# Two loads moved down the transfer queue in a fused spectral-and-MLP kernel

## The chip, the cores and the metric

The kernel runs on one core of one Trainium2 chip. The metric is device time in microseconds (us) for one execution. Before the change, three runs took 409.81, 409.92 and 409.93 us; the median is 409.92 us.

A core has five instruction queues, each of which works strictly in its own order: TensorE (PE, matmuls; its weight loads are listed apart as PEld), VectorE (DVE), ScalarE (ACT), GpSimd (POOL) and SyncE (SP). SP computes nothing here. It issues the transfers, all of them on one DMA queue that 16 DMA engines serve.

## The reference, cut to what matters

With `S = 2048` tokens and `D = 448` channels, `F = 1792`:

```python
xn  = layernorm(x)
A   = irfft2(rfft2(xn) * (w_r + 1j*w_i))          # spectral filter
h   = gelu(layernorm(xn) @ w1)                     # [S, D]
hs  = concat(shift(h, +1, -1, +2, -2)) @ w2        # one shift per quarter of the channels
x1  = xn + hs
B   = x1 + gelu(layernorm(x1) @ w3) @ w4           # w3 [D, F], w4 [F, D]
out = x + A + B
```

All of it is in float32. The kernel keeps the accuracy by splitting each float32 operand into a high and a low float16 half and multiplying three of the four products.

## The kernel before, in words

The 2048 tokens are seen as 128 rows of 16 blocks (token = 16 a + b); a block b holds the 128 tokens of one b. Four groups of four blocks are worked through in the order `GRP = [[14, 15, 0, 1], [2, 3, 4, 5], [6, 7, 8, 9], [10, 11, 12, 13]]`. The text calls them groups 0 to 3, as the code does.

The first 95 us are the front of the kernel:

- `norm1` normalises the blocks of a group. Groups 0 and 1 are transposed by TensorE (`turn_pe`, line 410). Groups 2 and 3 are split into halves by ACT and DVE and transposed by DMA (`turn`, line 900: source `x`, target `w4x`).
- `w1_unit(g, i)` (line 477) multiplies one block by w1 (`w1_in`, line 465, eleven matmuls), applies gelu on ACT (line 486), writes the high half on ACT (line 488) and the low half on DVE (line 489) into one of a few buffers `hs`, and lets SP transpose it into `h` (line 492). The text calls this last one a turning transfer of h. The diff calls them ("h", g, i).
- `w2_mm` and `w2_tile` (lines 498 and 514) multiply four shifted quarters of h by w2 (line 510, three matmuls for each quarter) and DVE adds the result to x (line 517).
- w3 and w4 each need one power-of-two scale for the whole matrix. `squares` (line 242) sums their squares on ACT (line 246), `powers` (line 248) adds up on DVE (line 251, tile `pt`), sums over partitions by one small TensorE matmul (line 258, tile `pm`), and makes the scale on DVE (lines 261 to 264). Then `split_w` writes the two halves (ACT line 291, DVE line 292). For w3 the text calls the sum pt3 and the matmul pm3, for w4 pt4 and pm4.

w3 has 448 rows. Three loads of 128 rows (line 217) and one of 64 rows (line 219) bring it into `w3raw`; the 64 rows are copied once more into the other 64 partitions by a transfer from `w3raw` to `w3raw` (line 1039).

After the front come the MLP (`front`, line 764: matmuls at line 435; `back`, line 791: matmuls at lines 811 and 826), and beside it the spectral path. Its first stage is `do_fold` (line 571): it reads two blocks of the original x again (line 574) into one of four buffers in turn. The fourth buffer, used by the folds of blocks 6 and 14, is the tile `hgm`, which is free from the start; the other three come into being only when earlier pools close.

The order on each queue is not the order of the code. A list scheduler with its own cost estimates sets it when the program is built. `behind(key)` (line 399) binds what is issued inside it to come after the instructions recorded under that key; for two transfers on SP this fixes their order. The program waits for data by semaphores, which the build places.

The chain of w4 touches the change as well. `load_w4` (line 231) brings w4 in four pieces; pieces 2 and 3 are issued behind ("h", 3, 3). Group 3 has only three `hs` buffers (`HS = 3`), so that its fourth block writes the buffer of its first, after that one's turning transfer has landed.

Of the kernel before, what the change touches and what calls it, by code (L numbers as in the profile page):

```python
# [19 lines left out]
S, D, DF, F = 2048, 448, 225, 1792  # L20
# [102 lines left out]
def body(tc, nc, x, wf, w1, w2, w3, w4, c_g, c_n, c_small, out):  # L123
    V, A, P, T, SY = nc.vector, nc.scalar, nc.gpsimd, nc.tensor, nc.sync
# [28 lines left out]
    def bank(tag, name):  # L153
        return ps.tile([128, 512], F32, tag=tag, bufs=2, name=name)
# [14 lines left out]
    xv = x.rearrange("(a b) d -> a b d", b=NB)  # L169
# [25 lines left out]
    def load_x(g):  # L195
        if g:
            SY.dma_start(xt[g], xv[:, GRP[g][0]:GRP[g][0] + 4])
        else:
            for i in (0, 2):
                SY.dma_start(xt[g][:, i:i + 2], xv[:, GRP[g][i]:GRP[g][i] + 2])  # L200
# [13 lines left out]
    def load_w3(ts):  # L214
        for t in ts:
            if t < 3:
                SY.dma_start(w3raw[:, t], w3[128 * t:128 * t + 128])
            else:
                SY.dma_start(w3raw[0:64, 3], w3[384:448])

    load_w3([0, 1])
    load_x(3)
    load_w3([2, 3])
    cross = x2mem.bitcast(F32)[:, 4 * F:4 * F + 2 * D].rearrange("p (i n) -> p i n", i=2)
    x2all = x2mem[:, 0:8 * F].rearrange("p (j t n) -> p j t n", j=4, t=7)
    w4raw = x2mem.bitcast(F32)[:, F:].rearrange("p (f n) -> p f n", f=14)
# [169 lines left out]
    after = {}  # L396

    @contextlib.contextmanager
    def behind(*key):
        key = key if len(key) > 1 else key[0]  # L400
        with contextlib.ExitStack() as st:
            for i in after[key]:
                st.enter_context(tc.issue_after(i))
            yield
# [51 lines left out]
    def h_at(g, i):  # L456
        return 128 * i if g else 144 * i + 16

    def w1_in(g, units, ts, passes=range(3)):
        for p in passes:  # L460
            for t in ts:
                for i, pm in units:
                    wi, xi = ((0, 0), (0, 4), (4, 0))[p]
                    if t < 3 or p != 1:
                        m = T.matmul(pm[:, :D], xTs[g][:, xi + t, 128 * i:128 * i + 128], w1p[:, wi + t],  # L465
                                     start=t == 0 and p == 0, stop=t == 3 and p == 2)
        return m
# [9 lines left out]
    def w1_unit(g, i, pm=None):  # L477
        if pm is None:
            pm = bank(("tr" if g < 3 else "mm", "acc")[i // 2], f"pw1_{g}{i}")
            after["u", g, i] = (w1_in(g, [(i, pm)], range(4)).ins,)  # L480
        c = CS[GRP[g][i]]
        pm = pm[:, :D]
        pv_ = pm.rearrange("p (k n) -> p k n", k=4)
        h = hs_buf[c % (HS if g == 3 else HS + 2)]
        with behind(0, max(i - 2, 0)) if g == 0 and i else contextlib.nullcontext():
            A.activation(out=pm, in_=pm, func=AF.Gelu_apprx_tanh, scale=gsc[:, c:c + 1])
        with behind("a2") if g == 1 and i > 1 else contextlib.nullcontext():
            u = A.activation(out=h[:, 0, :, 0:112], in_=pv_, func=AF.Copy, scale=h1)
            v = V.scalar_tensor_tensor(out=h[:, 1, :, 0:112], in0=pv_, scalar=h1, in1=h[:, 0, :, 0:112],
                                       op0=ALU.mult, op1=ALU.subtract)  # L490
        o = h_at(g, i)
        d = SY.dma_start_transpose(out=hT[g][:, :, o:o + 128], in_=h.rearrange("p i k n -> p (i k n)"))
        after[g, i] = u.ins, v.ins
        after["h", g, i] = (d.ins,)
# [3 lines left out]
    def w2_mm(b, ks):  # L498
        if b not in w2b:
            w2b[b] = bank("mm" if b in (2, 3) else "sp", f"pw2_{b}")  # L500
        for k in ks:
            src, o = b - SHIFT[k], 1
            if src < 0:
                src, o = src + NB, 0
            elif src >= NB:
                src, o = src - NB, 2
            g, i = WHERE[src]
            o += h_at(g, i) - 1
            for hi, wi in ((0, 0), (0, 1), (1, 0)):
                m = T.matmul(w2b[b][:, :D], hT[g][:112, 4 * hi + k, o:o + 128], w2p[:, wi, k],  # L510
                             start=k == 2 and hi + wi == 0, stop=k == 3 and hi == 1)
        after["w2", b] = (m.ins,)
# [58 lines left out]
    def do_fold(b0):  # L571
        f = xf_buf[b0 // 2 % 4]
        X = f.rearrange("p b s d -> p (b s d)")[:, 0:2 * D + 2].rearrange("p (b d) -> p b d", b=2)
        after["X", b0] = (SY.dma_start(X[:, :, 0:D], xv[:, b0:b0 + 2]).ins,)
        with behind("f", *FOLD[b0 // 2]):
            for i in range(2):
                x_ = X[:, i, 0:D]
                A.activation(out=x_, in_=x_, func=AF.Identity, scale=xn_scale[b0 + i], bias=xn_bias[b0 + i])
            A.activation(out=X[:, :, D:D + 1], in_=X[:, :, 0:1], func=AF.Copy)  # L579
        ad = X[:, :, 0:D].rearrange("p b (h d) -> p h b d", h=2)[:, :, :, 0:113]  # L580
        bc = X[:, :, 1:D + 1].rearrange("p b (h d) -> p h b d", h=2)[:, ::-1, :, 223:110:-1]
        u = xr.rearrange("p (a b s d) -> p a b s d", a=2, b=2, s=2)
        P.tensor_tensor(out=u[:, 0], in0=ad, in1=bc, op=ALU.add)  # L583
        P.tensor_tensor(out=u[:, 1], in0=ad, in1=bc, op=ALU.subtract)
        for k, op in ((0, ALU.add), (2, ALU.subtract)):
            i = P.tensor_tensor(out=f[:, :, k:k + 2].rearrange("p b s d -> p s b d"), in0=u[:, :, 0], in1=u[:, :, 1], op=op)
        after["fold", b0] = (i.ins,)
        for i in range(2):
            folds[b0 + i] = f[:, i].rearrange("p s d -> p (s d)")
# [429 lines left out]
    turn(2)  # L1019
    for k in range(1, 4):  # L1020
        w1_unit(1, k)
    for b, ks in ((0, (2,)), (1, (2,)), (0, (0,)), (2, (2,)), (1, (0,)), (2, (0,)), (3, (2,))):
        w2_mm(b, ks)
    with behind("w2p"):
# [86 lines left out]
    for b in range(0, NB, 2):  # L1111
        do_fold(b)
        step1_in(b)
        step1_in(b + 1)
        with behind("m", *PACE[b // 2]):
            step1(b)
            step1(b + 1)
# [80 lines left out]
```

## Time and profile before

| what | value |
|---|---|
| median of three runs | 409.92 us |
| the profiled execution, its own time | 409.72 us |
| its span in the trace | 407.6 us |
| PE busy | 401.3 us (98%) |
| DVE busy | 304.2 us (75%) |
| ACT busy | 268.6 us (66%) |
| POOL busy | 179.8 us (44%) |
| DMA queue | 46.4% of 16 engines' span |
| granted TensorE clock | 0.999 |

The trace counts 2.1 us less than the execution's time, for what lies before the first and after the last instruction. A row of the timeline has the start in us, the duration in us, the engine, the line, the operation, the tiles as out<-in, how many instructions are merged, and in square brackets how long the engine stood idle before it and what released it. In the list of transfers the last number is the time from issue to landing. A row of the table of stretches gives for each engine its busy time in the stretch, then the granted clock, the share of the DMA engines and what they moved in GB/s.

### The profile page before, as it was taken

To read this page: it belongs to the slowest core of one execution; us is meant where nothing else is said; L and a number is where in the kernel's file an instruction comes from. 1 tells how busy PE (TensorE), PEld (TensorE's weight loads), DVE (VectorE), ACT (ScalarE), POOL (GpSimd) and SP (SyncE) were. 2 spreads that over 40 slices of the span, in tenths; PEclk is the share of its full clock that TensorE was granted. 3 is DMA by queue.
4 is the path that set the end of the run, shared out by engine and by line. 5 is a ranking of instruction groups with operands and counts; after the bars stand their busy time and mean duration, and the time that the engine had idled before them with its cause. 6 is when DMAs were issued, how large, how long until landed. Compare 5 with 4: busy or idle time off the path is not lost.

```text
span 407.6 us, 8828 instructions
## 1 busy us (share of the span) xinstructions
PE 401.3 (98%) x3379; PEld 296.0 (73%) x3379; DVE 304.2 (75%) x658; ACT 268.6 (66%) x465; POOL 179.8 (44%) x276
## 2 busy tenths in 40 slices
PE   8998999999999999999999999999999999999996
PEld 4553555666767777776888887877788888888885
DVE  5988999899653757894577777763488879889645
ACT  4698993884737865763488888785956566544332
POOL 3889723011197747499243344441231254217100
PEclk9999999999999999999999999999999999999999
DMA  8999999915910375317055666642000022323201
GB/s 282 351 274 198 177 180 261 260 23 109 207 48 0 92 233 175 103 36 170 19 135 146 151 145 151 153 112 60 2 2 2 24 68 75 108 70 112 92 2 45
DMA packets 57209, 49.46 MB, mean 121 GB/s; under 512 B 41312, under 2 KB 52192, under 8 KB 57168
## 3 DMA queue, kind: packets, MB, share of 16 engines
q1 hardware_dynamic: 57168, 48.91, 46.4%
q8 instruction: 26, 0.43, 0.5%
q14 instruction: 15, 0.12, 0.1%
HBM read 35.06 MB, written 3.67 MB: 95 GB/s over the span
## 4 chain that ended last, share of the span: by engine, by line
PE 96%; DMA 2%; ACT 1%; DVE 0%; issue 0%; ACTq 0%
PE pw L435 33%; PE acc L811 24%; PE pw L510 9%; PE pw L465 6%; PE cr L826 4%; PE acc L826 3%; PE pu L707 3%; PE ps L604 3%; PE pp L661 2%; PE pe L727 2%; PE px L678 2%; PE py L749 2%; PE wps L889 2%; DMA h<-hs 2%; PE pta L414 1%; PE end L811 1%
## 5 line engine op out<-in xcount | busy, mean ns | idle before, releaser
L435 PE MATMUL pw<-x2mem,w3p 128*128 128x256 f16 x1232 | 149.7, 272 | 0.0
L435 PEld LDWEIGHTS <-w3p 128*128 128x128 f16 x1232 | 118.7, 98 | 19.4
L811 PE MATMUL acc<-w4p,hf 128*128 128x448 f16 x508 | 107.4, 352 | 0.0
L811 PEld LDWEIGHTS <-hf 128*128 128x128 f16 x532 | 51.5, 98 | 35.5
L777 DVE SCALAR_TENSOR_TENSOR hf<-pw,h,hf 128x512 f16<-128x512 f32 x56 | 41.8, 747 | 36.5 <-ACT hf L776 36.3
L773 ACT ACTIVATE pw<-pw,pe 128x512 f32<-128x512 f32 x56 | 36.7, 656 | 44.8 <-PE pw L435 44.6
L510 PE MATMUL pw<-w2p,h 112*128 112x448 f16 x192 | 39.2, 353 | 1.3 <-DMA h<-hs 1.2
L734 POOL TENSOR_TENSOR e<-e 128x226 f32<-128x226 f32 x16 | 11.1, 696 | 63.7 <-ACT e L731 56.2
L776 ACT ACTIVATE hf<-pw,h 128x512 f16<-128x512 f32 x56 | 38.3, 683 | 1.3
L465 PE MATMUL pw<-w1p,w4x 128*128 128x448 f16 x176 | 34.8, 352 | 0.5 <-DVE h L967 0.5
L510 PEld LDWEIGHTS <-h 112*128 112x128 f16 x192 | 18.4, 98 | 18.0 <-DMA h<-hs 2.2
L688 POOL TENSOR_TENSOR xr<-te 128x450 f32<-128x450 f32 x16 | 15.7, 981 | 34.5 <-DVE te L686 34.5
L465 PEld LDWEIGHTS <-w4x 128*128 128x128 f16 x176 | 17.1, 98 | 16.4 <-ACT w4x L424 0.7
L696 POOL TENSOR_TENSOR zb<-xr,zb 128x450 f16<-128x450 f32 x16 | 16.1, 1009 | 16.8 <-ACT zb L695 16.8
L684 DVE SCALAR_TENSOR_TENSOR te<-px,sc,wc 128x450 f32<-128x450 f32 x16 | 11.0, 685 | 10.6 <-ACT te L683 7.0
L683 ACT ACTIVATE te<-px 64x450 f32<-64x450 f32 x32 | 17.2, 538 | 1.7 <-PE px L678 1.2
L719 ACT ACTIVATE U<-y 113x512 f16<-113x512 f16 x32 | 18.0, 620 | 0.1
L741 ACT ACTIVATE vh<-e 128x448 f16<-128x448 f32 x16 | 9.2, 575 | 13.5 <-DVE e L739 13.3
L731 ACT ACTIVATE e<-pe 128x452 f32<-128x452 f32 x16 | 8.7, 545 | 14.0 <-PE pe L727 11.6
L540 POOL TENSOR_SCALAR y<-xt,nm 128x448 f32<-128x448 f32 x6 | 5.9, 986 | 23.3 <-DMA x2mem<-y 12.9
L711 DVE SCALAR_TENSOR_TENSOR y<-pu,y 113x512 f16<-113x512 f32 x16 | 10.9, 687 | 6.9 <-ACT y L710 6.8
L583 POOL TENSOR_TENSOR xr<-xf 128x452 f32<-128x452 f32 x6 | 6.7, 1125 | 20.6 <-ACT xf L579 10.5
(208 smaller groups left out, 799.0 us busy)
## 6 DMA issues: line engine op xcount, KB each, us to landing
wc<-wf SPq DMA_DIRECT2D x32, 225.0 KB, 3.8
wl<-wf SPq DMA_DIRECT2D x8, 450.0 KB, 3.9
xt<-x SPq DMA_DIRECT2D x3, 896.0 KB, 11.3
w3raw<-w SPq DMA_DIRECT2D x3, 896.0 KB, 14.6
xf<-x SPq DMA_DIRECT2D x6, 448.0 KB, 3.7
xr<-x SPq DMA_DIRECT2D x12, 224.0 KB, 2.5
out<-xr SPq DMA_DIRECT2D x12, 224.0 KB, 2.0
gn<-c_g SPq DMA_DIRECT2D x16, 128.0 KB, 3.2
```

The costliest lines, as they stand in the source:

```text
L435: m = T.matmul(ps_out, wp[:, wi + t, cols], xT[:, xi + t, tok], start=t == 0 and wi + xi == 0, stop=t == 3 and wi == 4)
L465: m = T.matmul(pm[:, :D], xTs[g][:, xi + t, 128 * i:128 * i + 128], w1p[:, wi + t], start=t == 0 and p == 0, stop=t == 3 and p == 2)
L510: m = T.matmul(w2b[b][:, :D], hT[g][:112, 4 * hi + k, o:o + 128], w2p[:, wi, k], start=k == 2 and hi + wi == 0, stop=k == 3 and hi == 1)
L683: i = A.activation(out=e[64 * h:64 * h + 64], in_=px_[64 - 64 * h:128 - 64 * h, :2 * DF], func=AF.Copy)
L688: P.tensor_tensor(out=z, in0=t[:, 0], in1=t[:, 1], op=ALU.add)
L696: P.tensor_tensor(out=zv[1], in0=z, in1=zv[0], op=ALU.subtract)
L719: A.activation(out=U[b][:113, p].rearrange("p q (c k) -> p q c k", c=NC), in_=Y1[:113, p, :, :, b], func=AF.Copy)
L773: A.activation(out=pm, in_=pm, func=AF.Gelu_apprx_tanh, scale=r3)
L776: i = A.activation(out=h[:, 0], in_=pv_, func=AF.Copy, scale=h3)
L777: j = V.scalar_tensor_tensor(out=h[:, 1], in0=pv_, scalar=h3, in1=h[:, 0], op0=ALU.mult, op1=ALU.subtract)
L811: m = T.matmul(to, h[:, hi, 2 * f + i], w4p[0][:, wi, 2 * fp + f, r], start=fp == s and f == 0 and hi + wi == 0, stop=fp == e and f == 1 a ...
L826: m = T.matmul(to, h[:, hi, slot] if slot < 4 else g[:, hi, slot - 4], w4f[fp][k][wi], start=k in (0, 6) and fp == 0 and hi == 0, stop=hi ...
```

## The change

The change moves two transfers down SP's queue and alters nothing that is computed.

- The 64-row piece of w3 was issued with the other three at the start (`load_w3([2, 3])`). It is now issued after the turning transfers of group 1, behind ("h", 1, 3).
- The row load of every fold is now bound behind ("h", 3, 3). Only the fold of blocks 6 and 7 (the fourth) was issued earlier than that before; it went out at the start, into `hgm`.

```diff
     load_w3([0, 1])
     load_x(3)
-    load_w3([2, 3])
+    load_w3([2])
...
     def do_fold(b0):
         f = xf_buf[b0 // 2 % 4]
         X = f.rearrange("p b s d -> p (b s d)")[:, 0:2 * D + 2].rearrange("p (b d) -> p b d", b=2)
-        after["X", b0] = (SY.dma_start(X[:, :, 0:D], xv[:, b0:b0 + 2]).ins,)
+        with behind("h", 3, 3):
+            after["X", b0] = (SY.dma_start(X[:, :, 0:D], xv[:, b0:b0 + 2]).ins,)
...
     for k in range(1, 4):
         w1_unit(1, k)
+    with behind("h", 1, 3):
+        load_w3([3])
     for b, ks in ((0, (2,)), (1, (2,)), (0, (0,)), (2, (2,)), (1, (0,)), (2, (0,)), (3, (2,))):
         w2_mm(b, ks)
```

Because the scheduler places everything anew, the built order moves elsewhere too. On SP, the changed kernel issues: three 128-row pieces of w3, the six turning transfers of h for blocks (0,0) to (1,1), the four of x for group 2, (1,2), (1,3), the 64-row piece of w3, (2,0), the copy from `w3raw` to `w3raw`, (2,1), three of x for group 3, two of line 553, the fourth of x, and then as before; the fourth fold's load stands directly behind that of the constants `csm`. On ACT, the squares of the 64-row piece stand four instructions later, behind the two of block (2,1) and the first cast of group 3's x. On DVE, `pt3` stands behind the end of a reciprocal root, block (2,1)'s low half and the split of the first block of group 3. On PE, 86 instead of 85 matmuls stand between the start of the w2 stage and pm3.

## The prediction

> **What bounds the kernel now.** I read the page's busy times first, then PE's waits, then the weight loads and matmuls of the stretch that has the wait.
>
> ```profile
> span 407.6 us, 8828 instructions
> PE 401.3 (98%) x3379; PEld 296.0 (73%) x3379; DVE 304.2 (75%) x658; ACT 268.6 (66%) x465; POOL 179.8 (44%) x276
> ```
>
> ```profile
> PE pw L510 <- DMA h<-hs: 1.2, 1, 1.2
> ```
>
> ```profile
> 32.07 0.30 PEld L510 LDWEIGHTS <-h 112*128 112x128 f16 x3 [1.61 <-DMA h<-hs]
> 32.94 0.87 PEld L510 LDWEIGHTS <-h 112*128 112x128 f16 x6 [0.57 <-DMA h<-hs]
> ...
> 35.30 1.44 PEld L510 LDWEIGHTS <-h 112*128 112x128 f16 x9 [0.35 <-DMA h<-x2mem]
> 37.18 2.00 PEld L510 LDWEIGHTS <-h 112*128 112x128 f16 x12 [0.44 <-DMA h<-x2mem]
> 39.35 8.16 PEld L465 LDWEIGHTS <-w4x 128*128 128x128 f16 x44 [0.16 <-DMA w4x<-x]
> ```
>
> ```profile
> 22.25 8.65 PE L465 MATMUL pw<-w1p,w4x 128*128 128x448 f16 x44
> 32.07 7.56 PE L510 MATMUL pw<-w2p,h 112*128 112x448 f16 x36 [1.17 <-DMA h<-hs]
> 39.47 8.49 PE L465 MATMUL pw<-w1p,w4x 128*128 128x448 f16 x44
> 47.79 0.92 PE L510 MATMUL pw<-w2p,h 112*128 112x448 f16 x4
> ```
>
> TensorE is the bound. Its only wait of a microsecond inside the run is at the start of the w2 stage, for turning transfers of h. The weight loads show the same wait five times in small. 44 matmuls from 39.47 to 47.79 give 0.189 us each without a stop. From 22.25 to 39.47 are 80 matmuls, 15.1 us at that pace, in 17.2 us. About 0.2 us of the difference lie before the w2 stage (a copy that DVE makes), so 1.9 us is all that better transfers can win here. From 39.47 on PE runs without a gap to 95 us.
>
> The cause of the wait is in SP's rows and in the landings.
>
> ```profile
> 25.04 6.80 SPq L492 DMA_TRANSPOSE h<-hs  x3
> ```
>
> ```profile
> 36.17 5.31 SPq L910 DMA_TRANSPOSE w4x<-x  x4
> 41.57 2.66 SPq L492 DMA_TRANSPOSE h<-hs  x2
> ```
>
> ```profile
> w3raw<-w SPq DMA_DIRECT2D x1, 448.0 KB, 18.3
> hgm<-x SPq DMA_DIRECT2D x1, 448.0 KB, 18.9
> ```
>
> ```profile
> 11.21 0.47 SPq L219 DMA_DIRECT2D w3raw<-w  x1
> 11.72 0.59 SPq L574 DMA_DIRECT2D hgm<-x  x1
> ```
>
> ```profile
> h<-hs SPq DMA_TRANSPOSE x1, 7.0
> ```
>
> ```profile
> 8.34 0.43 SPq L217 DMA_DIRECT2D w3raw<-w  x1
> ```
>
> ```profile
> w3raw<-w SPq DMA_DIRECT2D x1, 896.0 KB, 19.5
> ```
>
> The load ahead of the two moved ones lands at 8.34 + 19.5 = 27.8. The two moved loads land at 11.21 + 18.3 = 29.5 and 11.72 + 18.9 = 30.6. The first turning transfer, issued at 25.04 behind them, lands 7.0 later, at 32.0, where PE starts. Three issues take SP 6.80 us, while four of w4x take 5.31 (1.33 each).
>
> **The change part by part.** No instruction is added or removed; two transfers and the built order move.
>
> (1) *The queue's head.* Without the two loads the first turning transfer should land about 2.8 us earlier (30.6 less 27.8), near 29.2. PE ends its w1 work at 30.9, so the first wait goes; the next transfers follow at 1.3 each, under the 0.57 to 1.13 us that PE spends on each from a start 1.9 earlier. I take the whole 1.9 us as won up to the start of group 2.
>
> ```profile
> 32.13 0.63 ACT L488 ACTIVATE hs<-pw,h 128x448 f16<-128x448 f32 x1 [1.74 <-DMA h<-hs]
> ```
>
> ```profile
> 30.60 0.67 DVE L489 SCALAR_TENSOR_TENSOR x2mem<-pw,h,x2mem 128x448 f16<-128x448 f32 x1
> ```
>
> ACT waited 1.74 us for the same landing, so ACT and DVE behind it come about 1.7 earlier too.
>
> (2) *The fold's load* now follows `csm` at about 75 us, and delays the two transfers of line 553 behind it by 1.1 us, the time by which it landed after the w3 piece. They feed blocks 2 and 3, the MLP's second group, which PE reaches only after the seven slots of the first; the fold itself comes later still. Cost nothing; without that cover 1.1.
>
> (3) *The w3 piece.* The sixth transfer in SP's order, not moved, has its source when DVE ends at 31.27. From there SP issues the fifth and sixth, four of x, (1,2) and (1,3): eight at 1.33, so the piece is issued at about 42.1 instead of 11.2. Three things wait for it in strict order: the copy to the other partitions on SP, with (2,1) and group 3's x behind it; the squares on ACT; and through pt3 both DVE and PE. Before, that slack was 14 us; the squares ran at 43.22.
>
> ```profile
> 43.22 1.68 ACT L246 ACTIVATE xr<-w3raw 64x1792 f16<-64x1792 f32 x1
> ```
>
> ```profile
> 45.70 0.14 DVE L251 TENSOR_REDUCE pt<-m 128x1 f32<-128x5 f32 x1
> ```
>
> ```profile
> 48.74 0.28 PE L258 MATMUL pm<-pt,ones 128*128 128x1 f32 x2
> ```
>
> How late it lands is the unknown. Below: the first row load of the same 448 KB into an idle queue. Above: the copy of the same size between turning transfers.
>
> ```profile
> xt<-x SPq DMA_DIRECT2D x1, 448.0 KB, 3.5
> ```
>
> ```profile
> w3raw<-w3raw SPq DMA_DIRECT2D x1, 448.0 KB, 4.5
> ```
>
> ```profile
> 41.00:43.80 2.80, 2.80 (x16) 1.45 (x15) 2.63 (x13) 2.77 (x5) 0.64 (x4) 1.00 0.91 173
> 43.80:45.50 1.70, 1.70 (x10) 0.88 (x9) 1.56 (x6) 1.70 (x4) 1.70 (x3) 1.00 1.43 37
> 45.50:47.50 2.00, 2.00 (x12) 1.06 (x11) 1.93 (x7) 2.00 (x6) 1.91 (x5) 1.00 1.28 279
> ```
>
> So 45.6 to 46.6. I take 46.5, near the copy's row: two turning transfers stand ahead of the piece, and in just this place the table of stretches has a standstill, 37 GB/s for 1.7 us at full DMA share, after which transfers landed 4.3 to 4.8 after issue and not 3.1 to 3.5. The stretch holds one 16 KB packet of an instruction queue. If that packet belongs to a place in the program, it comes again, 1.9 us earlier, ahead of the w3 piece.
>
> ```profile
> q8 instruction: 1, 0.02, 3.5%
> ```
>
> The Trainium skill, page "Runtime: NRT & Kernel Launch", section "Instruction fetch mechanics", calls a 16 KiB refill mostly hidden. That row speaks against it for transfers under way; by the page the standstill would not recur, which is the first rival below.
>
> With 46.5: squares end at 46.5 + 1.8 = 48.3, pt3 at 48.4, pm3 at 48.5. PE free of stalls would be there at 47.0 (48.74 + 0.19 for one matmul more, less 1.9). So PE waits 1.5 and keeps 0.4.
>
> (4) *DVE carries the delay further.* DVE has no air here:
>
> ```profile
> 34.00:66.30 32.30, 32.29 (x174) 16.68 (x173) 31.93 (x80) 29.58 (x45) 19.15 (x51) 1.00 1.01 199
> ```
>
> ```profile
> 65.68 0.64 DVE L489 SCALAR_TENSOR_TENSOR hs<-pw,h,hs 128x448 f16<-128x448 f32 x1
> ```
>
> ```profile
> 70.05 0.63 ACT L488 ACTIVATE hs<-pw,h 128x448 f16<-128x448 f32 x1 [3.90 <-DVE nib L300]
> ```
>
> ```profile
> 79.81 0.95 ACT L246 ACTIVATE xr<-x2mem 128x896 f16<-128x896 f32 x1 [1.01 <-DMA x2mem<-w]
> ```
>
> ```profile
> 81.96 0.16 DVE L251 TENSOR_REDUCE pt<-m 128x1 f32<-128x8 f32 x1 [1.33 <-ACT xr L246]
> ```
>
> ```profile
> 82.39 0.28 PE L258 MATMUL pm<-pt,ones 128*128 128x1 f32 x2
> ```
>
> From pt3 (45.70) to the end of h(3,0)'s low half (66.32) DVE is busy for 20.6 us. In the changed order 2.6 us of that stand ahead of pt3 (root 1.35, split of x 0.67, low half of (2,1) 0.59), 0.65 come in (one statistics 0.53, one small 0.12), and I add 0.8 for two casts of x on ACT that now stand behind the late squares. So h(3,0) ends 19.45 after pt3: 48.35 + 19.45 = 67.8, 1.5 later than 66.32.
>
> From there a tight chain leads to pm4: the turning transfer of h(3,0) frees the buffer for (3,3) (ACT idle 3.90 until then), whose transfer lets the last w4 pieces go (ACT idle 1.01 for them), whose squares end in pt4 (DVE idle 1.33). Before, pt4 ended at 82.12 and PE reached pm4 at 82.39. Now pt4 ends at 83.6 and pm4 runs at 83.7, with 0.4 us of matmul work more behind PE than before (the built order puts it later by that). Net 83.7 - 82.39 - 0.4 = +0.9. PE's 0.4 gain of (3) is used up in waiting for pm4.
>
> **Sum.** 409.72 + 0.9 = 410.6 for the profiled execution; the median lies 0.2 above it, so 410.8.
>
> **The rivals.**
>
> *The piece lands as into an idle queue* (45.6, 0.9 earlier). Everything in (3) and (4) shifts with it one for one: no change, 409.9. For it: the 3.5 row, and a standstill that need not recur. Against: two turning transfers directly ahead. The Trainium skill, "DMA: Bandwidth & Descriptors", section "Anatomy of one DMA", gives 2.0 us and bytes over 436 GB/s, an estimate of 3.1 here; by it the time would be 409.5. The same-size rows, 3.5 and 4.5, are longer.
>
> *The other side: the squares never hold anyone.* If SP reaches the piece, or it lands, by about 44.6, pt3 follows DVE's own order, DVE keeps its 1.7 earlier start less 0.65, and pt4 comes about 0.5 before 82.12 or better. PE then keeps 1.1 or a little more of 1.9: 408.8. For it: PE's 1.9 us are real. Against: it needs a landing within 2.5 us of issue at 42.1, shorter than any row; it decides from 44.8 downwards.
>
> *The change does not empty the head*: the earlier w3 pieces alone could hold the first turning transfer past 30.9. Then the loss is that of (4) without (1): some 1.9 more, 412.7. They end near 27.8, so I give it little, and count it with slower.
>
> **How the numbers follow.** Forecast with its worse neighbours 0.45, idle-queue landing 0.35, squares hold no one 0.20. A measurement of this kernel tells about 0.2%, 0.8 us, from no change. Predicted is 410.8; its own range, by landings from 46.2 to 47.5, is 410.5 to 411.8. The range of all goes from 408.8, a little in, to 412.0: 409.0 to 412.0. Faster 0.20, same 0.35, slower 0.45.
>
> **What would show it.** Right: PE's wait at line 510 near 31 gone; the first turning transfer landing near 29; a PE wait of 1 to 2 us at pm3 with ACT idle before the 64-row squares for a transfer; a second PE wait at pm4; h(3,0)'s low half on DVE after 67. Wrong: the 64-row squares starting before 45, or pm4 without a wait.

## The result, and the profile after

The changed kernel takes 413.8 us, the median of six runs from 413.05 to 415.66. The kernel before takes 409.9 beside it. The ratio is 1.010, with a 95% interval from 1.008 to 1.013: slower by 1%, 3.9 us. The forecast was 410.8, within 409.0 to 412.0. The direction was right, the size was not. The profiled execution is the longest of the six, 415.66.

The head of the page, then the waits of PE, of the changed kernel:

```profile
span 413.7 us, 8827 instructions
PE 404.4 (98%) x3379; PEld 296.7 (72%) x3379; DVE 305.4 (74%) x658; ACT 268.6 (65%) x465; POOL 174.9 (42%) x276
```

```profile
PE pm L258 <- DVE pt L251: 3.4, 1, 3.4
```

The wait at line 510 that led this list is gone, and a wait of 3.4 us at pm3 has come. The weight loads and the matmuls of the same stretch as before (line numbers below the diff are one to three higher now):

```profile
30.79 6.72 PEld L510 LDWEIGHTS <-h 112*128 112x128 f16 x36
37.60 8.23 PEld L465 LDWEIGHTS <-w4x 128*128 128x128 f16 x44
```

```profile
30.98 6.98 PE L510 MATMUL pw<-w2p,h 112*128 112x448 f16 x36
37.79 8.49 PE L465 MATMUL pw<-w1p,w4x 128*128 128x448 f16 x44
46.12 1.30 PE L510 MATMUL pw<-w2p,h 112*128 112x448 f16 x6
50.81 0.59 PE L258 MATMUL pm<-pt,ones 128*128 128x1 f32 x2 [3.40 <-DVE pt L251]
...
87.86 0.28 PE L258 MATMUL pm<-pt,ones 128*128 128x1 f32 x2
```

All 36 weight loads now run as one row without a stop, where before there were five stops. PE starts group 2 at 37.79 and not at 39.47: 1.7 us won. At pm3 it stands 3.4 us, and pm4 comes at 87.86, 5.5 later than before, without a wait in this execution. Why pm3 waits is in ACT's and DVE's rows and in those of the transfers (start of the issue; then time from issue to landing):

```profile
48.78 1.70 ACT L246 ACTIVATE xr<-w3raw 64x1792 f16<-64x1792 f32 x1 [4.72 <-DMA w3raw<-w]
```

```profile
50.60 0.16 DVE L251 TENSOR_REDUCE pt<-m 128x1 f32<-128x5 f32 x1 [3.77 <-ACT xr L246]
...
69.45 0.68 DVE L489 SCALAR_TENSOR_TENSOR hs<-pw,h,hs 128x448 f16<-128x448 f32 x1
...
86.08 0.16 DVE L251 TENSOR_REDUCE pt<-m 128x1 f32<-128x8 f32 x1 [1.06 <-ACT xr L246]
```

```profile
39.76 3.56 SPq L492 DMA_TRANSPOSE h<-hs  x2
43.36 0.58 SPq L219 DMA_DIRECT2D w3raw<-w  x1
```

```profile
w3raw<-w SPq DMA_DIRECT2D x1, 448.0 KB, 5.4
h<-hs SPq DMA_TRANSPOSE x1, 4.1
```

ACT is idle for 4.72 us until the piece lands at 48.76. The squares follow, then pt3, then pm3. The chain of waits names the transfer itself:

```profile
43.36 5.39 DMA w3raw<-w
```

One thing was in no step of the prediction: the granted clock behind the wait. The third figure from the end is the clock.

```profile
42.00:43.70 1.70, 1.70 (x11) 0.88 (x10) 1.60 (x5) 1.67 (x4) 1.70 (x4) 1.00 1.32 35
```

```profile
50.30:57.10 6.80, 6.29 (x18) 2.83 (x19) 5.90 (x19) 6.80 (x14) 0.00 (x0) 0.50 0.94 180
```

From 50.3 TensorE runs at half clock for 6.8 us. In the 6.29 us of it in which PE is busy it gets 18 matmuls done, where 33 fit at 0.189: some 2.9 us lost. The first of the two rows is the standstill of the transfer queue, 35 GB/s for 1.7 us, which stood at 43.8 to 45.5 before. The start of the fold stage's first matmul shows how far PE has come: 676 matmuls lie ahead of it in both kernels.

```profile
119.09 1.50 PE L604 MATMUL ps<-csm,xh 128*128 128x128 f16 x24
```

```profile
124.14 1.50 PE L605 MATMUL ps<-csm,xh 128*128 128x128 f16 x24
```

Before it is 119.09, after 124.14: 5.05 of the 5.94 us between the two profiled executions (415.66 less 409.72) arise in the front. Most of the rest is lost near 382; the last section comes back to it.

### The profile page after: what moved, and what is told of

Same layout as the page of the kernel before. It is cut to its first block, busy times and chain, and to the rows that moved or that the text cites. A ratio compares the mean times of both kernels' runs of the same rounds, so it can differ in the third digit from the quotient of the medians.

```text
span 413.7 us, 8827 instructions
## 1 busy us (share of the span) xinstructions
PE 404.4 (98%) x3379; PEld 296.7 (72%) x3379; DVE 305.4 (74%) x658; ACT 268.6 (65%) x465; POOL 174.9 (42%) x276
## 3 DMA queue, kind: packets, MB, share of 16 engines
q1 hardware_dynamic: 57168, 48.91, 45.3%
## 4 chain that ended last, share of the span: by engine, by line
PE 79%; DVE 9%; ACT 3%; DMA 3%; issue 2%; SPq 0%; DVEq 0%; ACTq 0%
PE pw L435 28%; PE acc L812 22%; PE pw L510 8%; PE pw L465 4%; PE pu L708 3%; PE ps L605 3%; PE pp L662 2%; PE px L679 2%; PE cr L827 2%; PE acc L827 2%; DVE xr L560 2%; PE pe L728 1%; DMA out<-xr 1%; DMA w3raw<-w 1%; PE py L750 1%
## 5 line engine op out<-in xcount | busy, mean ns | idle before, releaser
L778 DVE SCALAR_TENSOR_TENSOR hf<-pw,h,hf 128x512 f16<-128x512 f32 x56 | 41.9, 748 | 38.3 <-ACT hf L777 38.1
L510 PE MATMUL pw<-w2p,h 112*128 112x448 f16 x192 | 41.6, 371 | 0.0
L510 PEld LDWEIGHTS <-h 112*128 112x128 f16 x192 | 19.7, 103 | 18.2 <-issue 3.5
L743 DVE TENSOR_TENSOR vh<-e,vh 128x448 f16<-128x448 f32 x16 | 10.9, 680 | 7.1 <-ACT vh L742 7.1
```

Of the source, the lines that this page charges most:

```text
L778: j = V.scalar_tensor_tensor(out=h[:, 1], in0=pv_, scalar=h3, in1=h[:, 0], op0=ALU.mult, op1=ALU.subtract)
```

## The experiments

Each expectation says what its own letters for theories mean. Only in the group on the late sum and the late queue do they stay the same from run to run: A is the late pt3, B the place in the queue, and C both, each enough by itself. All medians stand against runs of the kernel before on the same chip, 409.8 to 410.2.

### The two moves apart

`e1_fold_only`: the kernel before with the fold's load alone moved.

```diff
-        after["X", b0] = (SY.dma_start(X[:, :, 0:D], xv[:, b0:b0 + 2]).ins,)
+        with behind("h", 3, 3):
+            after["X", b0] = (SY.dma_start(X[:, :, 0:D], xv[:, b0:b0 + 2]).ins,)
```

> Only the fold's load is moved; the 64-row piece of w3 stays with the other three at the start. Theory A (the loss of the changed kernel is the late w3 piece, and the gain is the emptier head): the head is shorter by the 1.1 us that hgm took behind the w3 piece, the wait at the start of the w2 stage shrinks by about that, TensorE does not wait at pm3, and the time is 408.6 to 409.2. Rival B (moving the fold's load behind csm costs by itself, since it delays the transfers of line 553): 410 or more. Rival C (the head's backlog is worth nothing): 409.9.

`e2_w3_only`: the changed kernel with that edit taken back, so that only the piece of w3 is moved.

> Only the 64-row piece of w3 is moved; the fold's load stays at the start. Theory A: the first turning transfer still comes in time (about 30), pm3 waits for the late piece as in the changed kernel, 3 us or more, the granted clock drops to 0.5 behind that wait, and the time is 413.3 to 414.5. Rival (the two moves do their harm together): about 411.

Measured: 408.5 (408.1 to 409.8, ratio 0.997, interval 0.995 to 0.999) for the fold's load alone, just under the 408.6 to 409.2 of its Theory A, and 414.25 (413.2 to 414.8, ratio 1.009) for the piece alone. All PE waits over 0.3 us of the first:

```profile
PE wps L890 <- DVE x2mem L188: 1.2, 1, 1.2
PE pw L465 <- DVE h L968: 0.5, 1, 0.5
```

Both are older and lie in the first 15 us. In the second PE waits 3.4 at pm3 as in the changed kernel, and the half clock lasts 6.8 us there too. So the fold's load alone wins 1.3 us and beats both kernels, and the piece of w3 alone loses all that was lost. The two don't add up: on top of the moved piece the fold's load brings 0.45 (414.25 to 413.8), within the spread of either kernel's runs. The moved piece alone already lets the first turning transfer land at 29.49, in time for PE.

### The half clock

`e3_fill`: the changed kernel with sixteen idle matmuls ahead of pm3, so that PE doesn't stand long enough to lose its clock.

```diff
+            if key == "3":
+                for _ in range(16):
+                    T.matmul(pm[:, 64:512], w1p[:, 0, 0:128], w1p[:, 1], start=True, stop=True)
```

> The changed kernel with 16 matmuls of 448 columns added into unused columns of pm3's bank, where TensorE otherwise waits for pt3; the scheduler then leaves 5 more matmuls of the w2 stage (0.9 us) behind pm3. Theory A (half of the loss is the clock that the granted-clock row shows at 0.5 for 6.8 us after the wait): no drop of the clock, 3.1 us less and 0.9 more than the changed kernel, 411.2 to 412. Rival (the drop of the clock is not caused by the wait, or the time comes from the late pt3 alone): 413.8 or, with the 0.9, 414.7.

Measured: 414.8, granted clock 1.0 throughout. PE's waits:

```profile
50.59 0.38 PE L261 MATMUL pm<-pt,ones 128*128 128x1 f32 x2 [1.43 <-DVE pt L251]
...
87.40 0.38 PE L261 MATMUL pm<-pt,ones 128*128 128x1 f32 x2 [1.74 <-DVE pt L251]
```

The clock is saved and the time is not. What PE no longer loses at half clock it waits at pm4. This is the second wait of the prediction's step (4), hidden in the changed kernel only because PE was late itself. The run is not clean to the microsecond: the built order also moved five matmuls behind pm3, and pt4 ended 1.1 later (87.35 against 86.24). The changed kernel's own six executions point the same way: the one with a mean granted clock of 0.999, too high for a drop of 3.4 us, took 413.65, and the five at 0.991 to 0.996 took 413.05 to 415.66.

### Where the piece stands in the queue

Here `load_w3([3])` is bound elsewhere: behind ("h", 0, 3), between the fourth and fifth turning transfers (`e4_w3_mid`), or behind the four of x for group 2, ahead of (1,2) (`e8_before12`).

```diff
-    with behind("h", 1, 3):
+    with behind("h", 0, 3):        # e4_w3_mid
+    with behind("t", 2):           # e8_before12
         load_w3([3])
```

> The changed kernel with the 64-row piece of w3 issued behind the last turning transfer of group 0 instead of group 1, where SP has a gap of 0.7 us at 30.9. Theory A (what hurts is only that the piece lands after its readers need it): it lands near 35, eight us before the squares; the transfers behind it come 1 to 1.5 us later than in the changed kernel; no wait at pm3, and the time is 408.3 to 409.5. Rival (an ordinary load between turning transfers costs a standstill of the queue of 1.7 us or more wherever it stands, and TensorE waits for the next ones): 410 or more.

> The changed kernel, but the piece is issued two transfers earlier, ahead of (1,2) and behind the four of x for group 2. If a load lands 3.5 us after the turning transfer ahead of it has landed: near 43.6 to 44.5, the squares and pt3 stand where they stood in the kernel before. Theory A: no loss at pm3 or pm4; only (1,2) and (1,3) land some 3 us later, near 47.5 and 48.5, and PE may wait a microsecond for them: 409 to 410. Theory B: everything behind it comes 3 us later as in the changed kernel: 411.5 or more.

Measured: 410.2 and 413.3. There is no long wait at pm3 in either. In the first:

```profile
PE pw L510 <- DMA h<-x2mem: 2.0, 1, 2.0
```

```profile
w3raw<-w SPq DMA_DIRECT2D x1, 448.0 KB, 5.2
```

Behind the piece the next turning transfer lands at 37.44, 5.0 after the one ahead of it (32.47). PE's 2.0 us there give back the 1.5 to 1.9 us of the head, and the time is that of the rival, 410 or more. In four of its ten executions the granted clock averaged 0.996, and they took 411.6 to 411.8; the other six, at 0.999 or more, took 409.65 to 410.3. In the second kernel the piece, 6.6 us under way with the standstill in it, makes PE wait at 46.9 for (1,2). Its profiled execution, 411.55, is the shortest of ten, so it doesn't show what makes the median 413.3. Neither place was free.

### How much of it is bytes

`e7_half` and `e14_eighth` load only one half and one eighth of the piece's columns late; the rest goes with the first loads. The edit shown is that of the half; the eighth has `7 * F // 8` in place of `F // 2`.

```diff
     load_w3([2])
+    SY.dma_start(w3raw[0:64, 3, 0:F // 2], w3[384:448, 0:F // 2])
...
-        load_w3([3])
+        SY.dma_start(w3raw[0:64, 3, F // 2:F], w3[384:448, F // 2:F])
```

> The changed kernel, but only one half of the late piece's columns (224 KB) is loaded late; the other half goes with the first loads. The late part's landing against that of the turning transfer ahead of it (3.6 us in the changed kernel for 448 KB). If those 3.6 us are a fixed turn-around of the queue: again 3.3 to 3.6, and the time stays at 413.3 to 414. If they are the bytes: about 1.8, pt3 1.3 to 1.8 earlier, and the time 411.5 to 412.5. Between the two if both count.

> The changed kernel with one eighth of the late piece's columns (56 KB) loaded late and seven eighths with the first loads. Whole and half pieces landed 3.6 and 1.7 us after the turning transfer ahead of them. If the bytes set that distance: 0.5 or less, pt3 near 47.4, 3.2 earlier than in the changed kernel, and the time goes on falling with the landing (413.8, 412.4, then 410.4 to 411.3), with no PE wait of a microsecond at pm3. If a fixed turn-around of some 1.5 us is in it: lands 1.5 after (1,3), pt3 near 48.6, and 412 to 412.5 again.

The landing rows, of the half, then of the eighth:

```profile
w3raw<-w SPq DMA_DIRECT2D x1, 224.0 KB, 3.5
```

```profile
w3raw<-w SPq DMA_DIRECT2D x1, 56.0 KB, 2.7
```

| late part | (1,3) ahead lands | it lands | distance | next turning transfer lands after (1,3) | time |
|---|---|---|---|---|---|
| none (`e1_fold_only`) | 45.15 | | | 1.23 | 408.5 |
| 56 KB | 45.12 | 45.95 | 0.83 | 1.91 | 410.7 |
| 224 KB | 45.25 | 46.92 | 1.67 | 2.45 | 412.4 |
| 448 KB (changed kernel) | 45.17 | 48.76 | 3.59 | 4.36 | 413.8 |

The more bytes, the later the load lands behind the turning transfer ahead of it, and the longer the kernel takes: 2.8 us of landing and 3.1 us of time lie between an eighth and the whole. Not every step of the time is the landing's. Between the eighth and the half the fold stage begins only 0.5 later (120.16 and 120.63 in the profiles); of the 1.75 us between those two profiled executions 1.0 is lost near 380, as the last section says. Even 56 KB cost 2.2 us against no load there.

The single packets of the load show where its time goes. In all three kernels the first packet starts 1.4 us after the issue (44.73 in the changed kernel), right behind the last packets of (1,3); in the idle queue's row it starts 1.0 after it, and its first twelve take 0.2 to 0.9 us. Of the whole piece, the first twelve packets take 1.1 to 1.5 us each, while most of those that start from 46.0 to 46.3 take 0.27. The last one ends at 47.85 (whole), 46.19 (half) and 45.61 (eighth), and the landing comes 0.9, 0.7 and 0.3 later. What holds the first packets isn't shown.

With an eighth late PE's two waits are those that the prediction had described:

```profile
48.01 0.38 PE L259 MATMUL pm<-pt,ones 128*128 128x1 f32 x2 [0.75 <-DVE pt L252]
...
83.47 0.38 PE L259 MATMUL pm<-pt,ones 128*128 128x1 f32 x2 [0.80 <-DVE pt L252]
```

### Late sum or late queue

The piece does two things: pt3 waits for it, and SP's queue is held up, by the piece itself and by the copy of `w3raw` behind it, for whose source SP waits until 48.77 with (2,1) and x of group 3 behind it. `e5_no_sum` takes pt3's wait away (the 64 rows are left out of the sum), `e12_copy_late` moves the copy down in front of the w4 pieces, `e13_copy_late_no_sum` does both.

```diff
-    for k in range(4):                                                   # e5, e13
-        n = 128 if k < 3 else 64
-        with behind(*((1, 3), (1, 3), (1, 3), (2, 0))[k]):
-            squares(m3[:n, k:k + 1], w3raw[:n, k])
+    for k in range(3):
+        with behind(1, 3):
+            squares(m3[:, k:k + 1], w3raw[:, k])
```

```diff
-    with behind("h", 2, 0):                                              # e12, e13
-        SY.dma_start(w3raw[64:128, 3], w3raw[0:64, 3])
...
     with behind("t", 3), behind("h", 2, 3), behind("b0"):
+        SY.dma_start(w3raw[64:128, 3], w3raw[0:64, 3])
         for i in range(2):
             load_w4(i)
```

> The changed kernel, but the squares of the 64 late rows are left out of the sum for w3's scale (the scale is taken from 384 of 448 rows; the rows themselves are still loaded late, copied and split). So pt3 no longer waits for the late piece, while every transfer stands in the queue as in the changed kernel. Theory A (only the late pt3 costs: it goes on over DVE, h(3,0), the buffer, the last w4 pieces, pt4 to pm4): 408.3 to 409.3, as the kernel with the fold's load alone; no PE wait at pm3 or pm4. Theory B (the load's place among the turning transfers costs, because everything behind it in the queue comes some 3 us later): 411.5 or more.

> The changed kernel with the piece where it is in SP's queue, but its copy to the other partitions moved down, in front of the first w4 pieces. So SP no longer stands waiting for the piece's landing with (2,1) and x of group 3 behind it; pt3 is as late as in the changed kernel. Theory C: the late pt3 alone is enough, 413 to 414.5, with the 3.4 us PE wait at pm3. Theory B (the queue alone): the queue comes 1 to 2 us earlier behind the copy's old place, 411.5 to 412.5.

> Both: the copy moved down as in the run before, and the squares of the 64 late rows left out of the sum for w3's scale (which then comes from 384 of 448 rows). The piece itself still stands in SP's queue between the turning transfers. Theory C: both chains are relieved and only the piece's own time in the queue is left, some 3 us that the slack may or may not cover: 409 to 411, clearly below both single edits. If a third thing costs: 412.5 or more.

| | copy where it was | copy moved down |
|---|---|---|
| pt3 waits for the piece | 413.8 | 414.0 |
| pt3 doesn't wait | 413.9 | 411.5 |

The first of the three has pt3 at 41.05, and PE waits further on:

```profile
54.16 0.74 PE L510 MATMUL pw<-w2p,h 112*128 112x448 f16 x3 [1.59 <-DMA h<-x2mem]
55.46 2.06 PE L465 MATMUL pw<-w1p,w4x 128*128 128x448 f16 x7 [0.56 <-DMA w4x<-x]
```

That is (2,1) and x of group 3, behind the copy. In the second the old wait is there:

```profile
50.68 0.38 PE L258 MATMUL pm<-pt,ones 128*128 128x1 f32 x2 [3.51 <-DVE pt L251]
```

Either chain alone is enough for the whole loss; only both edits together bring something. My Theory A, a late pt3 as the only cause, fell with the first run: it expected 408.3 to 409.3. The last run stays 3.0 above the fold's load alone (2.5 when each is taken against the kernel before on its own chip), above the 409 to 411 of C, with waits of 0.4 to 0.9 us for h and for DVE (2.0 in all) and 1.0 us near 380, on which the last section has more. That the 2.0 come from the piece's own 3 us in the queue is likely, but was not tried alone.

Two runs tried the late sum without SP's queue. `e6_late_sum` is the fold's load alone with the 64 rows' squares taken from their second copy.

> The kernel with the fold's load alone moved (408.5), but the squares of the 64 rows are taken from their second copy in the other 64 partitions, which landed at 49.3 there. No transfer moves; only pt3 comes late, at about 51.2, as in the changed kernel (50.6) or a little later; the built order puts pm3 some 12 matmuls (2.3 us) further down on PE. Theory A (late pt3): h(3,0)'s low half ends some 19.4 after pt3, near 70.5, pt4 follows it by 16, near 86.5, PE waits at pm4: 412.5 to 414.5, with little wait at pm3 and no drop of the clock. Theory B (the load's place in the queue): nothing is moved there, 408.5 to 409.5.

Measured 414.8, but not for the reason given: the built order put a block of group 3 ahead of pm3, and PE stood 4.7 us for its x. It does not tell the theories apart.

```profile
53.39 0.93 PE L465 MATMUL pw<-w1p,w4x 128*128 128x448 f16 x2 [4.68 <-DMA w4x<-x]
```

`e11_act_copy_late` and `e9_act_queue` let ACT issue the piece on a queue of its own, near 41 with the copy moved down, and near 29.

```diff
-    with behind("h", 1, 3):
-        load_w3([3])
+    with behind(1, 1):             # e9_act_queue; e11_act_copy_late: behind(2, 0)
+        A.dma_start(w3raw[0:64, 3], w3[384:448])
```

> The piece on ACT's queue as above but issued after the high half of block (2,0), near 42, with the built order of the changed kernel; and its copy to the other partitions moved down SP's queue, in front of the first w4 pieces, so that SP waits nowhere for the piece. pt3 stays late, SP's queue doesn't: this is the late pt3 alone. It lands about 5 us after issue, near 47, squares end near 48.8. Theory C: pt4 follows pt3 by 35.5 as in the changed kernel, near 84.5, PE waits there: 410.8 to 412. Theory B (only the queue costs): 408.5 to 409.5.

> The changed kernel, but the late piece of w3 is issued by ACT on ACT's own transfer queue, after the high half of block (1,1), near 31, and no longer by SP between the turning transfers. Theory C (the piece costs in two ways, each enough by itself: everything behind it in SP's queue comes later, and pt3 comes later): neither is there, the piece lands by about 37, before its squares' turn; 408.3 to 409.5, no PE wait at pm3. If two queues disturb each other as much as one queue does (the 16 engines are the same): the turning transfers come some 3 us later as with the piece in the middle of SP's queue, 410 or more.

Measured: 410.8 and 414.6. In the first pt3 ends at 48.5, PE's waits between 46 and 84 us add up to 1.8, and the time is at the lower end of C's range; but (1,3) lands 2.4 later as well (47.33 against 44.95 in `e13_copy_late_no_sum`), so it isn't the late sum alone. The second (PE's row, then two transfers from issue to landing):

```profile
37.13 1.30 PE L510 MATMUL pw<-w2p,h 112*128 112x448 f16 x3 [3.51 <-DMA h<-x2mem]
```

```profile
w3raw<-w ACTq DMA_DIRECT2D x1, 448.0 KB, 7.5
h<-x2mem SPq DMA_TRANSPOSE x1, 7.9
```

The turning transfer (0,3), issued at 29.18, 0.08 us ahead of the piece on the other queue, lands 0.3 after it, at 37.08, where its like took 3.1 to 3.6. The second queue didn't help in either run. The Trainium skill, page "DMA: Bandwidth & Descriptors", section "Issuing engines are not separate DMA queues", says that all issuers share the same 16 engines; this pair of rows agrees.

## Why the prediction was right or wrong

**(1) The queue's head: right.** The first turning transfer landed at 29.0 (29.2 forecast), the wait at line 510 is gone, and PE was 1.7 earlier at group 2 (1.9 forecast). The fold's load alone already gets 1.5 of it at the fold stage (117.59 against 119.09).

**(2) The fold's load at no cost: right,** as `e1_fold_only` shows with no wait added.

**(3) The piece's landing: wrong, and this is the term that failed.** It was put at 46.5, between 45.6 and 46.6 (47.5 at the end of the forecast's own range), and came at 48.76. Two parts were mis-sized. The issue was put at 42.1 by eight issues of 1.33; it came at 43.36. The standstill did come again 1.8 earlier, as the prediction had feared, at the same 16 KB instruction packet, and the issues that met it were slow: the two ahead of the piece took 3.56 instead of 2.66. (Eight issues of 1.33 from 31.27 give 41.9, not 42.1; that is a small part.) The rest, 1.0 us, is the flight: 5.4 from the issue, where the prediction had 4.4 and, at most, the copy's 4.5. That bound was none: the copy moves within the chip's own buffers, and the piece is a load. The lower bound fitted no better. That load went into an idle queue and fills 128 rows, the piece 64; what the form is worth was not tried. The prediction's estimate of 3.1 has a flaw of its own: the Trainium skill, "DMA: Bandwidth & Descriptors", section "Anatomy of one DMA", gives its 2.0 us and 436 GB/s for transfers that GpSimd issues, and SP issues this one.

Seen afterwards, the landing of the transfer ahead gives a better figure: (1,3) had landed at 47.23 before, 45.3 with the 1.9 taken off, and with the 3.5 of the idle queue's row behind that the piece would have been put at 48.8. But that rule isn't shown. In every run with the piece in SP's queue its issue lay 1.6 to 1.9 us before the landing of the transfer ahead, so that the seven whole pieces other than that of `e8_before12` fit 5.2 to 5.5 from the issue just as well as 3.5 to 3.7 from that landing. Which of the two the next kernel should be reckoned by stays open.

**(4) DVE carries the delay on: right as a mechanism.** From the end of pt3 to the end of h(3,0)'s low half the forecast had 19.45; here it is 50.76 to 70.13, 19.4. pt4 came at 86.24; the forecast's 83.6 with the 2.4 that pt3 came later than forecast gives 86.0. The second wait at pm4 shows where PE isn't late by its clock (`e3_fill`, `e14_eighth`). Carrying the landing's 2.26 through to the end gives 410.8 + 2.3 = 413.1, which is the lower end of the six runs (413.05 to 415.66); the 0.7 that are missing to the median are not assigned. With an eighth of the piece late, landing at 45.95 and so 0.55 before the forecast's 46.5, the same chain gives pm4 at 83.15 and 410.25 us; measured are 83.47 and 410.7.

**What no step had.** The chain over SP's own queue was priced only in words ("with (2,1) and group 3's x behind it") and put at nothing; by `e5_no_sum` it is as long as the one over pt3, so a right landing time alone would not have made the account whole. And the half clock: behind the wait of 3.4 us PE lost some 2.9 more. The Trainium skill, "TensorE: Matmul & The Clock Gate", Part 1, has a rule on this: an idle window of about 3.4 us halves the clock. The profiled executions agree in the main: gaps of 3.4 to 4.7 dropped it for 3.4 or 6.8 us, and the single one of 2.0 (`e4_w3_mid`) did not. But the two of 1.6 and 0.6 close together in `e5_no_sum` did, for 3.4 us. In the changed kernel's profile at most 1.5 us of the loss can have counted: pm4 would have held PE until about 86.3, and it ran at 87.86.

Of the rivals, the landing as in an idle queue is refuted as it was meant, 3.5 from the issue; the 3.6 that was measured counts from the landing of (1,3). The squares that hold no one, and the head that isn't emptied, are refuted by the rows above.

## What to carry to other kernels

Don't price an ordinary load that goes between chained DMA transposes by its flight in an idle queue. Here 448 KB took 5.4 us from the issue, 3.6 from the landing of the transpose ahead, and put off the next transpose by 3.1; issuing it from another engine did not spare the transposes. Before moving a transfer down a queue, ask for every wait that comes to depend on it, the issuing engine's own included; if two chains carry the same delay, removing one alone can bring nothing, as here. Where an edit moves two things, run each alone: here one of them was the gain.

## What the runs showed of the hardware

- The same 448 KB cost the queue 0.9 us behind other ordinary loads (landings at 27.81 and 28.70 in `e1_fold_only`), and 3.1 us between two turning transfers (4.36 less 1.23).
- A 16 KB packet of an instruction queue came between 41 and 47 us in all fifteen profiles (43.85 before, 41.75 after, 41.72 in `e1_fold_only`, 43.10 in `e4_w3_mid`). In fourteen of them less than 60 GB/s were moved for 1.2 to 1.9 us from at most 0.6 us behind its start, with transfers under way; in `e9_act_queue`, where it came at 46.89 with no turning transfer under way, there was none to stand. That the packet is the cause, and doesn't only mark the place, was not tried.
- From the fold stage's first matmul to the end the profiles of six kernels (`e5_no_sum`, `e7_half`, `e11_act_copy_late`, `e12_copy_late`, `e13_copy_late_no_sum` and the changed one) take 289.5 to 289.6 us, and the others 288.4 to 288.6. In those six PE waits for DVE near 380 (0.28 and 0.42 near 382 and 384 in the changed kernel), behind one DVE instruction of line 743 that took 1.53 us where `e2_w3_only` has 1.10. The next one, of line 560, took 1.55 instead of 1.08, but so it did in seven of the profiles without the loss. The cause stays open, and whether it is what sets the profiled execution, 415.66, above the median can't be told.
